# A planned order of loads and blocks for the lead-in of chunked attention with a low-rank mixer and an MLP, replaced by another plan

## Chip, cores and metric

One NeuronCore of one Trainium2 chip. The metric is the device time of one launch in microseconds (us); lower is better.

## What is computed

`q`, `k`, `v` are (8, 8, 576, 64): batch, heads, sequence, head size. Attention runs inside chunks of 64 rows; its output feeds a mixer along the sequence (`U` is 576x32, `V` 32x576) and an MLP (512 to 2048 to 512). The mixer and MLP matrices arrive as 64-bit floats.

```python
scores = scale * np.matmul(q_c, k_c.transpose(0, 1, 2, 4, 3))   # per chunk of 64
attn = np.exp(scores - max) ; attn = attn / (sum + 1e-09)
x = (attn @ v_c)                                # as (batch, seq, 512)
h = x.transpose(0, 2, 1) @ U @ V
u = x + h.transpose(0, 2, 1)
out = u + np.maximum(u @ w_ch1, 0.0) @ w_ch2
```

## The kernel before, in words

Two batches make a pair (four pairs), and the 1152 rows of a pair are nine tiles of 128 rows, `T0` to `T8`. Three tiles are a group; a pair has groups 0, 1 and 2. Tiles 0 to 4 touch the pair's first batch, tiles 4 to 8 its second.

A tile's attention (`attention_ops`, L467): q and k are loaded by SP (L424, L425), v by POOL (L438); PE transposes q and k (L477) and ACT copies them out (L499); PE forms the scores `sc` (L507); VectorE takes maxima (L521) and subtracts (L526); ACT takes the exponential (L536); PE transposes (L477), ACT copies (L499), PE multiplies by v (`av`, L555), and VectorE divides by the sums (L567, L568, L574), which gives `x`.

The mixer: `y` is five products of a batch's `x` with U (L659), rounded to `ys` by ACT and VectorE (L674, L675). Per tile PE forms `u` from `ys` and V (L692), VectorE adds it to `x` (L698), PE transposes (`ut`, L704), ACT and VectorE write the high and low parts `uth` (L724) and `utl` (L729). Group 0 thus needs tiles 0 to 4, group 1 all tiles from 0 to 8.

The MLP runs in blocks. The hidden size is cut into 16 chunks of 128; chunk f has weights `W0` to `W15`. A block (`block_ops`, L801) is one chunk on one group: 12 hidden matmuls `h` (L757), a relu split by ACT (`hh`, L766) and VectorE (`hl`, L771), and 9 output matmuls `o` (L784), three for each of the three tiles, which add up in one PSUM bank per tile over all 16 chunks. Two groups in flight hold six of the eight banks.

A weight chunk arrives as 64-bit words (`wraw`, two transfers of 512 KB by SP, L327 and L331). ACT begins its conversion (L99), VectorE does six steps (L105, L106, L109, L112, L113, L114), ACT writes the high part (L350) and VectorE the low part (L353). The last three chunks are converted in halves. `U` and `V` are converted likewise; `V` also takes a round trip through four transfers by POOL (L296).

The lead-in is pair 0 up to the end of its groups 0 and 1, with the first two tiles of pair 1. Its order isn't written out: `Op` (L126) gives each piece an engine, a duration and a latency, and `order()` (L158) simulates them in time and emits the program in that order, choosing on each engine among the pieces that can start soonest the one with the lowest rank. The ranks come from the lists `LOADS` and `WORK` (L837, L838); `STRETCHES` (L839) is the order of the blocks as (group, first chunk, end chunk). `GATES` (L840) are the counts of blocks after which the first two tiles of pair 1 start; `HALVES_FROM` (L842) is the block from which one transfer a block copies q and k of pair 1 into a second layout (`halve`, L384, 8 for each batch), from which those tiles are then loaded. `begin_filling` and `fill` (L142, L148) put idle matmuls on PE where the plan leaves it without work. Every engine runs its own list strictly in order.

What follows pair 0's group 1 has an order written by hand.

Of the kernel before, what the change touches and what calls it, by code (L numbers as in the profile page):

```python
# [22 lines left out]
def kernel(  # L23
# [25 lines left out]
    GT = 3  # L49
# [108 lines left out]
    def order():  # L158
        free_at = {}
        stock = {k: [0.0] * n for k, n in ROOM.items()}  # L160
# [7 lines left out]
        out = []  # L168
        while ready:
# [29 lines left out]
            for u in users[o]:  # L199
                waits[u] -= 1  # L200
                if not waits[u]:
                    ready[u] = max(p.end + (p.lat if p.eng != u.eng or p.lat > 1 else 0.0) for p in u.after)
            out.append(o)
# [36 lines left out]
    def u_ops():  # L240
# [24 lines left out]

        ld = Op("POOL", 2.7, load, take="w", lat=2.0)
        o, _ = rounding(Later(lambda: st["raw"]), room, ld, "w", 10 * R)
        w = Op("ACT", 1.4, whole, o, take="w", free="w")
        h = Op("ACT", 1.8, high, w)
        lo = Op("DVE", 0.5, low, h, free="w")  # L270
# [7 lines left out]
    def v_ops():  # L278
# [26 lines left out]

        ld = Op("POOL", 0.7, load, take="w", lat=2.5)
        o, _ = rounding(Later(lambda: st["raw"]), room, ld, "w", n)
        o = Op("POOL", 2.4, spread, o, take="w", free="w w", lat=2.5)
        o = Op("ACT", 0.7, high, o)
# [12 lines left out]
    def w_ops(f, after=None):  # L322
# [12 lines left out]
        size = 2 * DM // n  # L335
        ld = Op("SP", 3.2, load, after, take="w", lat=2.0)
        halves = []
# [129 lines left out]
    def attention_ops(pr, t, *after):  # L467
# [102 lines left out]
        def scaled(e):  # L570
# [13 lines left out]
        lq = Op(  # L584
            "SP", 3.4 if own else 5.0, lambda: load_qk(pr, t), *after, take="w" if mine else "qk qk vn", lat=1.6
        )
        if own:
            tq = Op("PE", 0.55, lambda: transpose(src(0), "qT_"), lq, begun.get((pr, t - 2)), take="bank", free="" if mine else "qk")
        else:
            tq = Op("DVE", 1.09, lambda: squares(0, "qT_"), lq, begun.get((pr, t - 2)), take="qk", free="qk")  # L590
        lv = Op(
# [3 lines left out]
            lq,  # L595
            lat=2.2,
        )
# [7 lines left out]
        else:  # L605
            ck = Op("DVE", 1.09, lambda: squares(1, "kT_"), tq, take="qk", free="qk")
            turned = [[tq], [ck]]
# [6 lines left out]
        if own:  # L614
            te = Op("PE", 0.55, lambda: transpose(flat(), "eT_"), ex, take="bank", free=tag_e)
            ce = Op("ACT", 0.58, lambda: evacuate("eT_"), te, take=tag_eT, free="bank")
        else:
            te = Op("SP", 2.5, spread_e, ex, lat=4.0)
            ce = Op("DVE", 1.09, square_e, te, take="eT", free="e")
        av = Op("PE", 0.65, values, ce, lv, take="bank bank x", free=tag_eT + (" w" if mine else " vn"))  # L620
# [11 lines left out]
    def project_ops(pr, e, xs):  # L632
# [168 lines left out]
    def block_ops(pr, g, f, first, final, after, prev):  # L801
# [244 lines left out]
```

## Time and profile before

| | us |
|---|---|
| median of 3 runs | 941.47 |
| lowest and highest | 941.0, 941.57 |
| span of the profiled execution (first to last instruction) | 937.6 |
| PE busy in the span | 916.5 (98%) |
| VectorE busy | 488.7 (52%) |
| ACT busy | 212.3 (23%) |

The page gives the profiled execution's span and no separate time of its own; the median lies 3.9 us above the span. The shares are means over stages with different limits, so the lead-in has to be read by stretches.

### The profile page before, as it was taken

To read this page: it belongs to the slowest core of one execution; us is meant where nothing else is said; L and a number is where in the kernel's file an instruction comes from. 1 tells how busy PE (TensorE), PEld (TensorE's weight loads), DVE (VectorE), ACT (ScalarE), POOL (GpSimd) and SP (SyncE) were. 2 spreads that over 40 slices of the span, in tenths; PEclk is the share of its full clock that TensorE was granted. 3 is DMA by queue.
4 is the path that set the end of the run, shared out by engine and by line. 5 is a ranking of instruction groups with operands and counts; after the bars stand their busy time and mean duration, and the time that the engine had idled before them with its cause. 6 is when DMAs were issued, how large, how long until landed. Compare 5 with 4: busy or idle time off the path is not lost.

```text
span 937.6 us, 16153 instructions
## 1 busy us (share of the span) xinstructions
PE 916.5 (98%) x6639; PEld 806.1 (86%) x6642; DVE 488.7 (52%) x922; ACT 212.3 (23%) x379; POOL 30.1 (3%) x84
## 2 busy tenths in 40 slices
PE   7789999999999999999999999999999999999998
PEld 4569999878898888888898898988889889999997
DVE  6789999975545535553434534553433643321211
ACT  5434343322211212121211221111121211111110
POOL 5510000000000000000000000000000000000000
PEclk9999999999999999999999999999999999999999
DMA  9980688546646535563543733562231512310000
GB/s 214 222 260 1 140 168 185 138 129 146 143 98 150 127 57 130 124 127 81 129 92 79 153 70 79 150 140 68 78 91 35 148 45 46 79 23 1 35 1 34
DMA packets 271449, 98.79 MB, mean 105 GB/s; under 512 B 221296, under 2 KB 257136, under 8 KB 271376
## 3 DMA queue, kind: packets, MB, share of 16 engines
q1 hardware_dynamic: 269440, 94.81, 44.5%
q0 software_dynamic: 1328, 2.80, 1.4%
q8 instruction: 52, 0.85, 0.4%
q10 hardware_dynamic: 608, 0.15, 0.1%
q14 instruction: 21, 0.17, 0.1%
HBM read 73.84 MB, written 37.75 MB: 119 GB/s over the span
## 4 chain that ended last, share of the span: by engine, by line
PE 91%; DMA 3%; DVE 3%; issue 1%; ACT 1%; SPq 0%; POOL 0%; DVEq 0%; ACTq 0%
PE h L757 43%; PE o L784 41%; DMA qkv<-in_q_dram 2%; PE av L555 2%; PE sc L507 2%; PE u L692 1%; PE y L652 1%; PE y L653 1%; DMA vall<-vroom 1%; PE y L659 1%; PE ps_fill L151 0%; DVE eT L463 0%; PE ps_qT L477 0%; DMA us<-us_3d 0%; PE ps_kT L477 0%
## 5 line engine op out<-in xcount | busy, mean ns | idle before, releaser
L757 PE MATMUL h<-uth,w 128*128 128x384 f32 x1536 | 413.5, 337 | 1.6 <-DVE ex L528 1.6
L784 PE MATMUL o<-w,hh 128*128 128x512 f32 x1152 | 346.6, 393 | 0.0
L757 PEld LDWEIGHTS h<-uth,w 128*128 128x128 f32 x1536 | 279.8, 188 | 10.6 <-issue 1.4
L757 PE MATMUL h<-utl,w 128*128 128x384 f32 x768 | 258.1, 336 | 1.3 <-DVE utl L729 1.3
L784 PEld LDWEIGHTS o<-w,hh 128*128 128x128 f32 x1152 | 213.8, 188 | 36.7
L784 PE MATMUL o<-w,hl 128*128 128x512 f32 x576 | 214.2, 396 | 0.0
L771 DVE SCALAR_TENSOR_TENSOR hl<-h,hh 128x384 fp32r<-128x384 f32 x192 | 105.5, 549 | 203.3 <-ACT hh L766 202.8
L766 ACT ACTIVATE hh<-h 128x384 fp32r<-128x384 f32 x192 | 94.4, 491 | 458.7 <-PE h L757 458.5
L757 PEld LDWEIGHTS h<-utl,w 128*128 128x128 f32 x768 | 144.1, 188 | 7.9 <-DVE utl L729 1.6
L784 PEld LDWEIGHTS o<-w,hl 128*128 128x128 f32 x576 | 107.4, 188 | 22.9
L463 DVE STREAM_TRANSPOSE uT<-us 128x512 f32<-128x512 f32 x27 | 29.6, 1097 | 50.7 <-PE h L757 26.9
L463 DVE STREAM_TRANSPOSE eT<-es 128x512 f32<-128x512 f32 x27 | 29.1, 1079 | 41.0 <-DMA es<-es_6d 9.5
L463 DVE STREAM_TRANSPOSE qT<-qn 128x512 f32<-128x512 f32 x27 | 19.1, 709 | 46.4 <-PE h L757 44.7
L536 ACT ACTIVATE ex<-ex 128x512 f32<-128x512 f32 x36 | 22.8, 634 | 72.4 <-DVE ex L528 60.2
L641 ACT CAST xh<-x 128x512 fp32r<-128x512 f32 x30 | 18.5, 618 | 69.7 <-DVE x L574 44.7
L698 DVE TENSOR_TENSOR x<-u,x 128x512 f32<-128x512 f32 x36 | 24.2, 685 | 19.2 <-PE u L692 19.0
L521 DVE TENSOR_REDUCE mx<-sc 128x4 f32<-128x256 f32 x72 | 27.9, 413 | 5.4 <-PE sc L507 5.4
L724 ACT CAST uth<-uT 128x512 fp32r<-128x512 f32 x27 | 16.7, 620 | 53.6 <-DVE uT L463 53.6
L574 DVE TENSOR_TENSOR x<-av,sm 128x256 f32<-128x256 f32 x72 | 27.2, 419 | 1.4 <-DMA out_dram<-x 0.3
L414 POOL MEMSET vn<- 128x8 f32 x27 | 3.1, 114 | 689.1 <-PE av L555 506.3
L796 DVE TENSOR_TENSOR x<-o,x 128x512 f32<-128x512 f32 x36 | 23.1, 677 | 3.6 <-PE o L784 3.6
L645 DVE TENSOR_TENSOR xl<-x,xh 128x512 fp32r<-128x512 f32 x30 | 20.6, 686 | 7.6 <-ACT xh L641 6.8
(85 smaller groups left out, 531.7 us busy)
## 6 DMA issues: line engine op xcount, KB each, us to landing
wraw<-in_moe_w_ch_dram SPq DMA_DIRECT2D x32, 512.0 KB
out_dram<-x SPq DMA_DIRECT2D x36, 256.0 KB
halfq<-in_q_dram SPq DMA_DIRECT2D x24, 288.0 KB
halfk<-in_k_dram SPq DMA_DIRECT2D x24, 288.0 KB
qn<-halfq SPq DMA_DIRECT2D x27, 256.0 KB
kn<-halfk SPq DMA_DIRECT2D x27, 256.0 KB
vn<-in_v_dram SPq DMA_DIRECT2D x108, 64.0 KB
qkv<-in_v_dram POOLq DMA_DIRECT2D x36, 64.0 KB, 7.3
```

The source lines that it names most:

```text
L463: turned = nc.vector.transpose(dst, src)
L507: nc.tensor.matmul(ps[e][cs, hp * C : (hp + 1) * C], lhsT=st["qT_"][rows, hp, cs], rhs=st["kT_"][rows, hp, cs], start=True, stop=True,)
L521: nc.vector.reduce_max(mx, st["sc"][e], axis=AX.X)
L536: nc.scalar.activation(exf, exf, AF.Exp, scale=SCALE)
L574: nc.vector.tensor_mul(by_head[:, heads(pr, t, e), :], st["av"][e][:, :, 0:D], st["sm"][:, e].unsqueeze(2).broadcast_to([P, HP, D]),)
L645: nc.vector.tensor_sub(st["l"], x_of[pr, i + 4 * e], st["h"])
L698: nc.vector.tensor_add(x, st["u"], x)
L757: o = nc.tensor.matmul(ps[:, :GN], lhsT=w[:, z, cc], rhs=u[:, cc, :], start=(n == 0), stop=(n == 3 * NCC - 1))
L766: nc.scalar.activation(hh, ps[:, :GN], AF.Relu)
L771: nc.vector.scalar_tensor_tensor(hl, ps[:, :GN], 0.0, hh, op0=ALU.max, op1=ALU.subtract)
L784: nc.tensor.matmul(acc[g, j], lhsT=h[:, js], rhs=w2[f][:, z], start=(first and i == 0), stop=(final and i == 2),)
L796: nc.vector.tensor_add(x, ps, x)
```

## The change

The program is made by the same planner with other durations, another account of transfers and other lists. No instruction that computes is added or removed; 11 idle matmuls are added in all (53 in place of 42). The core of the diff:

```diff
     class Op:
-        def __init__(self, eng, us, run, *after, take="", free="", lat=0.1):
-            self.eng, self.us, self.run, self.lat = eng, us, run, lat
+        def __init__(self, eng, us, run, *after, take="", free="", lat=0.1, dma=0.0):
+            self.eng, self.us, self.run, self.lat, self.dma = eng, us, run, lat, dma
...
-        free_at = {}
+        free_at = {"SP": 1.85, "POOL": 1.4, "ACT": 3.4, "DVE": 1.5, ("SP", "dma"): 3.9, ("POOL", "dma"): 2.0}
...
-            free_at[o.eng] = end
+            free_at[o.eng] = end - (0.08 if o.eng in ("DVE", "ACT") else 0.0)
+            if o.dma:
+                first = max(t + 1.2, free_at[o.eng, "dma"])
+                other = "SP" if o.eng == "POOL" else "POOL"
+                both = min(o.dma, max(0.0, free_at[other, "dma"] - first))
+                end = free_at[o.eng, "dma"] = first + o.dma + both
+                if both:
+                    free_at[other, "dma"] += both
...
-        ld = Op("SP", 3.2, load, after, take="w", lat=2.0)
+        ld = Op("SP", 1.1, load, after, take="w", dma=3.55, lat=2.2)
...
-    STRETCHES = ((0, 0, 2), (1, 0, 2), (0, 2, 3), (1, 2, 3), (0, 3, 4), (1, 3, 4), (0, 4, 5), (1, 4, 5), (0, 5, 6), (1, 5, 6), (0, 6, 7), (1, 6, 7), (0, 7, 8), (1, 7, 8), (0, 8, 9), (1, 8, 9), (0, 9, 10), (1, 9, 10), (0, 10, 11), (1, 10, 11), (0, 11, 12), (1, 11, 12), (0, 12, 13), (1, 12, 13), (0, 13, 14), (1, 13, 14), (0, 14, 16), (1, 14, 16))
+    STRETCHES = ((0, 0, 4), (1, 0, 1), (0, 4, 5), (1, 1, 6), (0, 5, 6), (1, 6, 8), (0, 6, 8), (1, 8, 11), (0, 8, 9), (1, 11, 12), (0, 9, 16), (1, 12, 16))
-    GATES = (25, 27)
+    GATES = (23, 28)
...
-    HALVES_FROM = 8
+    HALVES_FROM = 16
...
-                Op("SP", 0.6, second.pop(0), prev[0], lat=3.0)
+                halved.append(Op("SP", 0.8, second.pop(0), prev[0], dma=2.75, lat=2.0))
...
-                attention_ops(1, gates[blocks], prev[0])
+                attention_ops(1, gates[blocks], prev[0], *halved[:8])
```

`LOADS` and `WORK` are new lists of the same items, and the loop over `WORK` now makes its pieces in a fixed order and takes only the rank from the list. About twenty durations change by some tenths of a us.

What comes of it on SP, the queue of the early loads: before, W0, T1, T0, T3, T4, W1, T2, T5, T8, W2, T6, T7, W3; now W0, T0, T2, T1, T3, W1, T4, T5, W2, T6, T8, T7, W3. On POOL the round trip of V now stands ahead of all v loads; before, it stood between those of T2 and T5.

On ACT, around the start of the conversion of chunk 2 (`L99`; `ex_5` is the exponential of tile 5, `qkT_6` a copy of tile 6). Before:

```order
L536 ACTIVATE ex_5_604<-ex_5_604 128x512
L299 CAST vst<-vall 128x576
L99 ACTIVATE wroom_675<-wraw_562 128x1024
L499 COPY eT_5_680<-ps_eT_5_667 128x512
L536 ACTIVATE ex_8_672<-ex_8_672 128x512
```

Now:

```order
L543 ACTIVATE ex_3_455<-ex_3_455 128x512
L99 ACTIVATE wroom_558<-wraw_161 128x1024
L506 COPY qkT_5_574<-ps_qT_5_561 128x512
L506 COPY eT_3_578<-ps_eT_3_552 128x512
L506 COPY qkT_5_574<-ps_kT_5_568 128x512
L543 ACTIVATE ex_4_549<-ex_4_549 128x512
L357 CAST w_625<-wroom_389 128x1024
```

Chunk 2 is begun two tiles earlier in the attention, ahead of copies that tiles 3 and 5 need.

On PE, at the first hidden matmul (`y_1` is the second batch's product with U, `u_4` and `ut_4` tile 4's mixer steps). Before:

```order
L659 MATMUL y_1_566<-x_8_794,ust_147 128x512
L704 MATMUL ut_2_949<-ident,x_2_714 128x128 x4
L704 MATMUL ut_3_957<-ident,x_3_441 128x128 x4
L692 MATMUL u_4_964<-ys_0_842,vst 128x512
L692 MATMUL u_4_964<-ys_1_954,vst 128x512
L692 MATMUL u_5_968<-ys_1_954,vst 128x512
L757 MATMUL h_0_0_977<-uth_0_900,w_245 128x384
L757 MATMUL h_0_0_977<-utl_0_901,w_245 128x384
```

Now, the end of the first hidden block, and a piece some rows later:

```order
L771 MATMUL h_0_0_948<-utl_0_865,w_281 128x384
L771 MATMUL h_0_0_948<-uth_0_864,w_281 128x384
L484 MATMUL ps_eT_8_968<-ident,ex_8_908 128x128 x4
L673 MATMUL y_1_906<-x_7_962,ust_142 128x512
L562 MATMUL av_0_8_983<-qkv_8_221,eT_8_977 64x65 x2
```

```order
L798 MATMUL o_0_1002<-w_625,hl_0_1_1046 128x512
L706 MATMUL u_4_1072<-ys_0_784,vst 128x512
L706 MATMUL u_4_1072<-ys_1_1062,vst 128x512
L706 MATMUL u_5_1075<-ys_1_1062,vst 128x512
L798 MATMUL o_1_1011<-w_625,hh_0_1_1041 128x512 x2
L798 MATMUL o_1_1011<-w_625,hl_0_1_1046 128x512
L798 MATMUL o_2_1015<-w_625,hh_0_1_1041 128x512 x2
L798 MATMUL o_2_1015<-w_625,hl_0_1_1046 128x512
L718 MATMUL ut_4_1089<-ident,x_4_714 128x128 x4
L718 MATMUL ut_5_1095<-ident,x_5_796 128x128 x4
```

The first hidden block now stands ahead of the end of tile 8 and of the second batch's mixer, which follow between blocks.

On PE, after the scores of pair 1's first tile. Before:

```order
L507 MATMUL sc_1_0_1939<-kT_0_1928,qT_0_1923 64x64 x2
L757 MATMUL h_1_13_1968<-uth_1_970,w_1801 128x384
L757 MATMUL h_1_13_1968<-utl_1_971,w_1801 128x384
L757 MATMUL h_1_13_1968<-uth_1_970,w_1801 128x384 x2
L757 MATMUL h_1_13_1968<-utl_1_971,w_1801 128x384
```

Now:

```order
L514 MATMUL sc_1_0_1925<-kT_0_1919,qT_0_1910 64x64 x2
L798 MATMUL o_1_1011<-w_1724,hh_0_13_1902 128x512 x2
L798 MATMUL o_1_1011<-w_1724,hl_0_13_1905 128x512
L798 MATMUL o_2_1015<-w_1724,hh_0_13_1902 128x512 x2
L798 MATMUL o_2_1015<-w_1724,hl_0_13_1905 128x512
L771 MATMUL h_0_14_1953<-uth_0_864,w_1786 128x384
```

Output matmuls now stand between the scores and the next hidden block. Chunk 15's first block is the 28th of 32 in place of the 30th. From the third group's third hidden block on, PE's order is the same in both programs.

## Rows read from the trace of the kernel before

**Rows 1.** Busy time by stretch of the span: the columns, then the stretches.

```profile
core 0: us, PE busy (x) PEld busy (x) DVE busy (x) ACT busy (x) POOL busy (x), PEclk, DMA share, GB/s
...
40.00:50.00 10.00, 7.37 (x147) 5.88 (x149) 7.13 (x19) 6.14 (x11) 4.80 (x10) 0.85 1.21 213
...
60.00:68.30 8.30, 6.18 (x52) 3.25 (x51) 7.77 (x16) 3.33 (x6) 0.00 (x0) 1.00 0.61 215
68.30:85.70 17.40, 17.39 (x91) 15.88 (x92) 17.11 (x22) 6.22 (x10) 0.00 (x0) 1.00 0.06 23
85.70:165.00 79.30, 79.30 (x406) 72.51 (x405) 76.10 (x95) 30.29 (x41) 0.00 (x0) 1.00 0.71 147
165.00:182.00 17.00, 16.81 (x112) 14.61 (x110) 15.88 (x30) 5.60 (x11) 0.00 (x0) 1.00 0.66 153
```

**Rows 2.** Timeline of PE at the first hidden matmul: start us, us, what.

```profile
66.71 0.33 PE L757 MATMUL h<-uth,w 128*128 128x384 f32 x1
68.31 0.44 PE L757 MATMUL h<-utl,w 128*128 128x384 f32 x1 [1.26 <-DVE utl L729]
```

**Rows 3.** Who PE waited for: us in total, times, longest us.

```profile
PE h L757 <- DVE ex L528: 1.6, 2, 1.1
...
PE u L692 <- DVE x L698: 0.8, 1, 0.8
```

**Rows 4.** DMA queues, 0 to 39 us (q1 SP, q0 POOL): packets, MB.

```profile
q1 hardware_dynamic: 17028, 6.46, 82.9%
q0 software_dynamic: 808, 1.74, 20.4%
```

**Rows 5.** DMA queue of SP, 0 to 8 us and 0 to 41 us.

```profile
q1 hardware_dynamic: 1785, 1.31, 52.7%
...
q1 hardware_dynamic: 17466, 6.99, 83.2%
```

**Rows 6.** Timeline of ACT: the conversions of chunks 0 and 2 begin.

```profile
9.73 1.12 ACT L99 ACTIVATE wroom<-wraw 128x1024 f32<-128x1024 f32 x1 [2.72 <-DMA wraw<-in_moe_w_ch_dram]
...
44.29 1.12 ACT L99 ACTIVATE wroom<-wraw 128x1024 f32<-128x1024 f32 x1 [2.04 <-DMA wraw<-in_moe_w_ch_dram]
```

**Rows 7.** VectorE by line and shape, 0 to 75 us: count, busy, ns.

```profile
L521 DVE TENSOR_REDUCE mx<-sc 128x4 f32<-128x256 f32 x18 | 7.5, 418 | 4.5 <-PE sc L507 4.4
L574 DVE TENSOR_TENSOR x<-av,sm 128x256 f32<-128x256 f32 x18 | 6.8, 419 | 0.3
...
L698 DVE TENSOR_TENSOR x<-u,x 128x512 f32<-128x512 f32 x6 | 3.8, 680 | 0.0
L109 DVE SCALAR_TENSOR_TENSOR wroom<-wraw,wroom 128x1024 uint32<-128x1024 uint32 x3 | 3.7, 1219 | 0.0
...
L105 DVE TENSOR_SCALAR wroom<-wroom 128x1024 f32<-128x1024 f32 x3 | 2.1, 690 | 1.2 <-ACT wroom L99 1.2
L567 DVE TENSOR_SCALAR sm<-av 128x4 f32<-128x4 f32 x18 | 2.1, 155 | 3.8 <-PE av L555 3.8
L568 DVE RECIPROCAL sm<-sm 128x8 f32<-128x8 f32 x9 | 1.8, 203 | 0.3
```

**Rows 8.** Timeline of VectorE in the dense stretch: two neighbours.

```profile
102.00 1.22 DVE L353 TENSOR_TENSOR w<-wroom,w 128x1024 fp32r<-128x1024 f32 x1
103.13 1.22 DVE L109 SCALAR_TENSOR_TENSOR wroom<-wraw,wroom 128x1024 uint32<-128x1024 uint32 x1
```

**Rows 9.** Timeline of PE, 50 to 67 us: the small products.

```profile
57.56 0.70 PE L555 MATMUL av<-qkv,eT 64*64 64x65 f32 x32
...
59.05 0.60 PE L477 MATMUL ps_eT<-ident,ex 128*128 128x128 f32 x4
...
62.76 1.98 PE L659 MATMUL y<-x,ust 128*128 128x512 f32 x4 [0.47 <-DVE x L574]
...
66.13 0.74 PE L692 MATMUL u<-ys,vst 128*128 128x512 f32 x2 [0.29 <-DVE ys L675]
```

**Rows 10.** Timeline of VectorE: the last steps of chunk 15.

```profile
189.77 1.25 DVE L353 TENSOR_TENSOR w<-wroom,w 128x512 fp32r<-128x512 f32 x2
```

More of the change, by code (lines that the diff above doesn't have):

```diff
@@ L201, in order @@
                 if not waits[u]:
-                    ready[u] = max(p.end + (p.lat if p.eng != u.eng or p.lat > 1 else 0.0) for p in u.after)
+                    ready[u] = max(p.end + (p.lat if p.lat > 0.1 and p.eng != u.eng or p.lat > 1 else 0.1 if "PE" in (p.eng, u.eng) and p.eng != u.eng else 0.03) for p in u.after)
             out.append(o)
@@ L264, in low @@
             nc.vector.tensor_sub(ust[:, :, 3, :], st["u"].bitcast(F32), ust[:, :, 3, :])
-        ld = Op("POOL", 2.7, load, take="w", lat=2.0)
+        ld = Op("POOL", 0.0, load, take="w", lat=5.0)
         o, _ = rounding(Later(lambda: st["raw"]), room, ld, "w", 10 * R)
-        w = Op("ACT", 1.4, whole, o, take="w", free="w")
-        h = Op("ACT", 1.8, high, w)
+        w = Op("ACT", 1.15, whole, o, take="w", free="w")
+        h = Op("ACT", 1.5, high, w)
         lo = Op("DVE", 0.5, low, h, free="w")
@@ L304, in low @@
             nc.vector.tensor_sub(dst, st["all"][rows], dst)
-        ld = Op("POOL", 0.7, load, take="w", lat=2.5)
+        ld = Op("POOL", 0.7, load, take="w", dma=0.6, lat=2.2)
         o, _ = rounding(Later(lambda: st["raw"]), room, ld, "w", n)
-        o = Op("POOL", 2.4, spread, o, take="w", free="w w", lat=2.5)
+        o = Op("POOL", 2.2, spread, o, take="w", free="w w", dma=1.0, lat=2.0)
         o = Op("ACT", 0.7, high, o)
@@ L584, in attention_ops @@
         lq = Op(
-            "SP", 3.4 if own else 5.0, lambda: load_qk(pr, t), *after, take="w" if mine else "qk qk vn", lat=1.6
+            "SP",
+            (1.0 if own else 0.8) * len(list(segments(pr, t))),
+            lambda: load_qk(pr, t),
+            *after,
+            take="w" if mine else "qk qk vn",
+            dma=2.5 if own else 2.3,
+            lat=2.2,
         )
@@ L589, in attention_ops @@
         else:
-            tq = Op("DVE", 1.09, lambda: squares(0, "qT_"), lq, begun.get((pr, t - 2)), take="qk", free="qk")
+            tq = Op("DVE", 0.71, lambda: squares(0, "qT_"), lq, begun.get((pr, t - 2)), take="qk", free="qk")
         lv = Op(
@@ L595, in attention_ops @@
             lq,
-            lat=2.2,
+            dma=1.45,
+            lat=2.0,
         )
@@ L605, in attention_ops @@
         else:
-            ck = Op("DVE", 1.09, lambda: squares(1, "kT_"), tq, take="qk", free="qk")
+            ck = Op("DVE", 0.71, lambda: squares(1, "kT_"), tq, take="qk", free="qk")
             turned = [[tq], [ck]]
@@ L617, in attention_ops @@
         else:
-            te = Op("SP", 2.5, spread_e, ex, lat=4.0)
-            ce = Op("DVE", 1.09, square_e, te, take="eT", free="e")
+            te = Op("SP", 0.7, spread_e, ex, dma=2.0, lat=3.5)
+            ce = Op("DVE", 0.9, square_e, te, take="eT", free="e")
         av = Op("PE", 0.65, values, ce, lv, take="bank bank x", free=tag_eT + (" w" if mine else " vn"))
@@ L676, in out @@
             y_of[pr, e] = y
-        y = Op("ACT", 1.4, out, prev, take="y", free="bank")
+        y = Op("ACT", 0.6, out, prev, take="y", free="bank", lat=0.8)
         steps[-1].append(y)
@@ L815, in out @@
             st[j] = project_out(pr, g, f, (st["hh"], st["hl"]), first, final, j)
-        a = Op("PE", 2.1, h, *after, *(prev[:1] + prev[3:] if prev else ()), take="bank", free="ut" if last else "")
+        a = Op("PE", 2.085, h, *after, *(prev[:1] + prev[3:] if prev else ()), take="bank", free="ut" if last else "")
         a.name = "hidden"
@@ L823, in block_ops @@
         for j in range(GT):
-            d = Op("PE", 0.7, lambda j=j: out(j), c, d, take="bank" if first else "", free="h" if j == GT - 1 else "")
+            d = Op("PE", 0.69, lambda j=j: out(j), c, d, take="bank" if first else "", free="h" if j == GT - 1 else "")
             if final:
@@ L850 @@
     mixed = {}
-    for item in WORK:
-        rank[0] += 1
+    for item in sorted(WORK, key=lambda z: ("UVTWPM".index(z[0]), int(z[1:] or 0))):
+        rank[0] = 1 + WORK.index(item)
         begin = len(ops)
@@ L878 @@
     blocks = 0
+    halved = []
     second = halvings(2) + halvings(3)
```

5 lines of the change are left out of this document (3 added, 2 removed).

## Prediction

> **What bounds the kernel.** The table by stretches comes first [rows 1]. From 85.7 to 165 us PE is busy for all of 79.3 us, so nothing can be won there except by starting earlier; what can be won lies in the 68.3 us before the first hidden block runs, and in the change to pair 1. In the lead-in the DMA engines are full (share 1.21 from 40 to 50 us) and VectorE is not far from it (7.13 of 10 us there, 7.77 of 8.3 us just before 68.3). Then the timeline of PE: the first hidden matmul starts at 66.71, and the second, the first that reads `utl`, waits until 68.31 for VectorE [rows 2]. So VectorE's list up to the third `utl` of group 0 sets the start. Last the waits of PE: two before a hidden block for the subtraction `ex`, 1.6 us, and one of 0.8 us for `x`, all at the entry to pair 1 [rows 3].
>
> The sum is made against the profiled span of 937.6 us; the median of 941.47 lies 3.9 us above it, and I add that back. About 0.2%, 1.9 us, is what a measurement here can tell from no change.
>
> **Term A, the start of the hidden blocks.** Chunk 2 decides it. Ahead of it on SP now stand U, W0, W1 and six tiles (before, seven), so it is complete when SP's queue has moved 6.44 MB; POOL has by then moved the words of V, its round trip and five tiles' v, 1.75 MB. Before, that sum, 8.2 MB, was reached at 39 us [rows 4]. Between the count and the use there is a delay: chunk 2's 6.96 MB were counted by 41 us [rows 5] and ACT began at 44.29, 3.3 us later; chunk 0's 1.19 MB were counted before 8 us and ACT began at 9.73, at least 1.7 us later [rows 5, 6]. I take 2.6, about the middle, and keep both ends. ACT starts at 41.6 and needs 1.1 us: 42.7.
>
> From there VectorE has 46 instructions up to the third `utl`: 21 of the attention's 256-column kind (maxima, subtractions, scalings) at 0.42, 8.8 us; four triples for the sums at 0.51, 2.1; eight of 512 columns (`ys`, four additions, three `utl`) at 0.68, 5.4; three steps of a chunk at 0.69 and two at 1.22, 4.5 [rows 7]. That is 20.8 us of durations. Neighbours that don't depend on each other overlap: the step at 102.00 lasts 1.22 and the next starts 1.13 later [rows 8], 0.09 less. The new list alternates between such neighbours; I count 29 overlaps, 2.6 us, so 18.2. One wait comes on top: behind chunk 2 on ACT stand two copies that tile 3's `av` needs, so that product ends about 1.1 us after VectorE has done its first step. Sum 42.7 + 18.2 + 1.1 = 62.0, against 68.3: **6.3 us earlier**. Ends: with the delay at 1.7 and no wait 60.0 (8.3 earlier); with 3.3 and no overlap at all 65.3 (3.0 earlier).
>
> The Trainium skill's page DMA: Bandwidth & Descriptors (Anatomy of one DMA) puts the fixed part of a DMA, most of it the receipt of the last byte, at about 2.0 us. By that figure ACT would start 0.6 us sooner and the forecast would be 938.2 instead of 938.8. Chunk 2's own row shows 3.3, so the sum stays with rows.
>
> **Term B, what moves behind the first hidden block.** Before, only `ut_4` and `ut_5` came after it. Now also tile 8's transpose of the exponential (0.60), its `av` (0.70), two `y` products (1.98 for four), and three `u` products (0.74 for two) [rows 9]: 0.55 + 0.65 + 1.0 + 0.7, a little under the rows since they overlap, **2.9 us later**. This is work moved, not added; it has to be paid after the start instead of before.
>
> **Term C, new waits among the first blocks.** Before, the stretch from 68.3 to 85.7 is full (17.39 of 17.40 us) [rows 1], so any wait is new. After the third `utl`, VectorE has eight more instructions before tile 8's exponential can start (a subtraction, a 1.14 step of chunk 2, the sums, maximum, scalings): 3.0 us, and ACT 0.65. The hidden block ends 1.9 us after that `utl`, so PE waits 1.75. `u_4` needs `ys_1`, behind chunk 3's step on VectorE: 0.55. `ut_4` and `ut_5` need two additions that stand behind two steps and a relu: 0.8. In all **3.1 us later**. Where the trace has no such row I bound it: 0.5 if VectorE is ahead of my count by one long step each time, 5 if chunk 4's load or conversion is late too.
>
> A + B + C leave 0.3 us at the place that was 85.7 us (four hidden and four output blocks done; now five and three, the same work).
>
> **Term D, the entry to pair 1.** The scores take the two free PSUM banks, and the next hidden block waits until a subtraction frees one: 1.6 us twice, and 0.8 for `u` behind `u` [rows 3]. Now two output groups (1.4 us) and four (2.8 us) stand between, and output products stand between the `u`; a maximum and a subtraction need 0.8 [rows 7]. I take all **2.4 us as gone**; the other end is 0.
>
> Everything else at nothing: the idle matmuls run where PE has no data; the halving transfers, moved from block 8 to block 16, run beside a DMA share of 0.71 [rows 1], and the last of a batch's eight is wanted some 10 us after its issue. If that cover fails, the first tile of pair 1 is late and PE waits at its scores. V's round trip, now early, no longer delays tile 5's v; its cost is already in the 1.75 MB.
>
> Sum: -6.3 + 2.9 + 3.1 - 2.4 = -2.7. Span 934.9, time **938.8 us**.
>
> **Rivals.**
> *More is won.* If chunk 2 lands early and VectorE never waits, A is 8.3; with C at 1.5 the sum is -8.3 + 2.9 + 1.5 - 2.4 = -6.3: 935.2. For it: the new order is built on transfers that share engines, which these rows show. Against it: the delay of chunk 2 in its own row. 0.16.
>
> *The plan doesn't hold, nothing is won.* ACT stands in order behind each chunk's load; the plan placed it where it thought the chunk had landed. If chunk 2 is used 2 us later than I have it, A is 4.3, and the sum -0.7: 940.8; if the entry to pair 1 also keeps its waits, +1.7: 943.2. For it: ACT did wait 2.04 us for chunk 2 before [rows 6]. 0.21.
>
> *Slower: VectorE becomes the bound.* Chunk 15 is now wanted two blocks earlier, and chunks 2 and 3 right behind the start. Before, VectorE ended chunk 15 at 191.0 [rows 10]. Now it is about 5.4 us ahead at the place of 85.7, lays 4.4 us of pair 1's first two tiles and seven relus (3.2) behind, and loses 4.3 us of idle (3.2 and 1.1, [rows 1]): chunk 15 at 173.7, with a relu behind it that PE wants at about 173. There is no room. If half of the some 80 overlaps up to there and half of the 29 before are missed (3.6 and 1.3 us), VectorE is 4.9 us later, and with the 0.7 that is already short the sum is -2.7 + 5.6 = +2.9: 944.4. It decides from about 0.04 us more for each step. Against it: the lists alternate between independent steps more than before. The Trainium skill's page VectorE: DVE Perf Modes (The DRAIN you can't avoid) says that the next instruction doesn't start until the pipe has emptied. By that rule no neighbours overlap, all 109 overlaps at 0.09 are missed, 9.8 us, and the time would be about 949; the 1.13 of [rows 8] speaks against it for independent neighbours, and I give that whole size 0.02 of the 0.13 that slower gets.
>
> **Chances.** Forecast case, 936.9 to 940.9: 0.50, two thirds of it below 939.6. More won 0.16, nothing won 0.21, slower 0.13. Faster by over 0.2%: 0.34 + 0.16 = 0.50; within: 0.16 + 0.21 = 0.37; slower 0.13. The range leaves out the outer part of the first and last rival: 934.5 to 944.5; the forecast case alone has 936.9 to 940.9.
>
> **What would show it.** In the profile after: ACT's start on chunk 2 near 41.6 with a wait on DMA ahead of it; the second hidden matmul near 62; small waits of PE on VectorE, some 3 us together, between there and 86; no wait on `ex` at the entry to pair 1; PE's waits between 86 and 170 near nothing. I am wrong if chunk 2 starts more than 2 us off, if PE waits on `hl` or on a chunk (`w`) in the dense stretch, or if the scores of pair 1's first tile wait for its loads.

## The result and the profile after

The changed kernel takes **949.47 us** (median of 4 runs, 948.7 to 951.01) against 941.24 us for the kernel before (median of 4, 940.02 to 941.57): a ratio of 1.0089, 95% interval 1.0072 to 1.0106. Forecast were 938.8 us and a range of 934.5 to 944.5. The sign is wrong, and the time lies outside the range.

The profiled execution after has a span of 949.2 us and took 951.01 us itself, so 1.8 us lie around the span. The prediction had taken 3.9 us for that distance; by 1.8 us, the profiled execution of before (937.6 us) took 939.4 us and was a short one. The two traces are therefore 11.6 us apart and the medians 8.2.

The stretches of [rows 1] and one behind them, in the kernel after:

```profile
core 0: us, PE busy (x) PEld busy (x) DVE busy (x) ACT busy (x) POOL busy (x), PEclk, DMA share, GB/s
40.00:50.00 10.00, 7.41 (x142) 6.08 (x142) 4.78 (x14) 6.32 (x10) 2.63 (x5) 0.66 1.10 230
60.00:68.30 8.30, 7.71 (x93) 5.38 (x93) 7.79 (x20) 4.46 (x8) 0.11 (x1) 1.00 0.41 120
68.30:85.70 17.40, 17.09 (x114) 13.95 (x113) 16.10 (x26) 7.78 (x11) 0.00 (x0) 1.00 0.35 121
85.70:165.00 79.30, 79.15 (x396) 70.90 (x395) 78.56 (x106) 29.42 (x42) 0.00 (x0) 1.00 0.46 116
165.00:182.00 17.00, 17.00 (x115) 15.07 (x114) 12.80 (x25) 4.82 (x9) 0.11 (x1) 1.00 0.75 109
182.00:210.00 28.00, 24.11 (x175) 20.53 (x174) 14.19 (x29) 5.30 (x10) 0.11 (x1) 0.94 0.69 138
```

From 40 to 50 us, where the forecast let VectorE run through, it is busy for 4.78 us (before: 7.13), and the granted clock of TensorE is 0.66, which between 2.4 and 1.2 GHz means some 6.8 us at the lower level (before, 0.85: 3 us). PE had stood idle for 3.2 us just ahead of it. The timelines of PE and ScalarE say why:

```profile
42.59 1.15 PE L562 MATMUL av<-qkv,eT 64*64 64x65 f32 x32 [3.18 <-ACT eT L506]
```

```profile
34.99 0.63 ACT L543 ACTIVATE ex<-ex 128x512 f32<-128x512 f32 x1 [1.59 <-DVE ex L533]
40.46 1.12 ACT L99 ACTIVATE wroom<-wraw 128x1024 f32<-128x1024 f32 x1 [4.84 <-DMA wraw<-in_moe_w_ch_dram]
41.48 0.58 ACT L506 COPY qkT<-ps_qT 128x512 f32<-128x512 f32 x1
41.94 0.60 ACT L506 COPY eT<-ps_eT 128x512 f32<-128x512 f32 x1
```

ScalarE stands 4.84 us before chunk 2 (2.04 in [rows 6]), and the copies of tiles 3 and 5 that PE and VectorE need stand behind it in its order. At the start of the hidden blocks (the timeline of PE, as in [rows 2]):

```profile
64.83 1.20 PE L562 MATMUL av<-qkv,eT 64*64 64x65 f32 x30 [0.47 <-DMA qkv<-in_v_dram]
...
66.91 0.74 PE L771 MATMUL h<-uth,w 128*128 128x384 f32 x1
67.48 0.34 PE L771 MATMUL h<-utl,w 128*128 128x384 f32 x1
...
89.25 0.62 PE L798 MATMUL o<-w,hh 128*128 128x512 f32 x2
```

The first product that reads `utl` is 0.8 us earlier than before, not 6.3. In the kernel before it started as soon as the third `utl` was written [rows 2]; here it did not wait for it. VectorE's timeline:

```profile
63.35 0.68 DVE L743 TENSOR_TENSOR utl<-ut,uth 128x512 fp32r<-128x512 f32 x1
```

The third `utl` is there at 64.03, and the product that reads it runs 3.45 us later: ahead of it in PE's order stand the rest of a batch's `y`, tile 7's values product `av`, held until 64.83 by the load of v, a transposition and more of `y`. At 89.25 us five hidden and three output blocks are done, the same amount of products as four and four at 85.70 us before.

The third loss is at the entry to pair 1, here on VectorE, ScalarE and PE, one timeline each:

```profile
194.45 0.64 DVE L712 TENSOR_TENSOR x<-u,x 128x512 f32<-128x512 f32 x1
200.58 0.75 DVE L581 TENSOR_TENSOR x<-av,sm 128x256 f32<-128x256 f32 x2 [5.49 <-DMA out_dram<-x]
```

```profile
201.37 0.62 ACT L655 CAST xh<-x 128x512 fp32r<-128x512 f32 x1 [9.40 <-DVE x L581]
201.89 0.48 ACT L780 ACTIVATE hh<-h 128x384 fp32r<-128x384 f32 x1
```

```profile
202.43 1.22 PE L798 MATMUL o<-w,hh 128*128 128x512 f32 x2 [3.89 <-ACT hh L780]
```

VectorE waits 5.49 us until a buffer of pair 0 is stored; ScalarE's next step reads what VectorE writes, a relu stands behind it, and PE waits 3.89 us for that relu. The waits of [rows 3] on `ex` are gone, and this one has taken their place. (The 1.22 for two products is the lower clock again: 0.94 in the stretch.)

To compare programs whose blocks stand in another order I use PE's **lag**: every product counts with its spacing at the full clock (0.1735 us for one of a hidden block, 0.229 for one of an output block, and so on; idle matmuls count nothing), and the lag is how much later than in the profiled execution of before the same sum is reached. It is worked out from all rows of PE, and belongs to one execution of each kernel. At 70 us, where the orders still differ in small products, the spacing taken for those shifts it by some 0.6 us.

| lag in us at | 70 | 100 | 160 | 200 | 260 | 600 | 900 |
|---|---|---|---|---|---|---|---|
| after | 2.9 | 3.6 | 4.9 | 8.0 | 9.5 | 10.8 | 11.6 |

So in these traces the lead-in costs 3.6 us, the dense stretch 1.3, the entry to pair 1 4.6 and the rest 2.

### The profile page after: what moved, and what is told of

It is laid out like the page before. It is cut to its first block, busy times and chain, and to the rows that moved or that the text cites. A ratio compares the mean times of both kernels' runs of the same rounds, so it can differ in the third digit from the quotient of the medians.

```text
span 949.2 us, 16174 instructions
## 1 busy us (share of the span) xinstructions
PE 924.3 (97%) x6653; PEld 810.3 (85%) x6653; DVE 482.9 (51%) x922; ACT 210.4 (22%) x379; POOL 30.2 (3%) x84
## 4 chain that ended last, share of the span: by engine, by line
PE 81%; DMA 6%; DVE 6%; SPq 3%; issue 2%; ACT 1%; POOL 1%; DVEq 0%; ACTq 0%; POOLq 0%
PE h L771 38%; PE o L798 37%; DMA qkv<-in_v_dram 2%; PE av L562 2%; PE sc L514 2%; PE y L666 1%; DVE wroom L109 1%; PE y L667 1%; PE u L706 1%; SPq L461 1%; DVE hl L785 1%; DVE wraw L113 1%; DMA us<-us_3d 1%; DMA vall<-vroom 1%; DVE w L360 1%
## 5 line engine op out<-in xcount | busy, mean ns | idle before, releaser
L562 PEld LDWEIGHTS av<-vn,eT 64*64 64x64 f32 x864 | 15.8, 134 | 12.0 <-issue 12.0
```

Source lines behind the costliest of these rows:

```text
L562: nc.tensor.matmul(ps[e][cs, hp * D1 : (hp + 1) * D1], lhsT=st["eT_"][rows, hp, cs], rhs=vn[rows, c, hp, :], start=True, stop=True,)
```

## The experiments

Times are medians; the ratio is to the kernel before, run on the same chip in turn. The planner makes its order anew for each edit, so most edits move more than the line that they change; where that matters, the text says how many of PE's 5443 matmul instructions (idle ones not counted) stand elsewhere in the program, as a comparison of the two lists counts them.

| run | what | us | ratio, 95% |
|---|---|---|---|
| e1_halves8 | after, halving transfers from block 8 | 946.09 | 1.0054, 1.0039 to 1.0069 |
| e2_chunk2_later | after, chunk 2 planned to land later | 951.63 | 1.0106, 1.0088 to 1.0123 |
| e3_both | e1 and e2 | 948.41 | 1.0081, 1.0062 to 1.0100 |
| e4_before_halves16 | before, halving transfers from block 16 | 949.98 | 1.0093, 1.0076 to 1.0111 |
| e5_v7_early | e3, v of tile 7 earlier | 944.23 | 1.0026, 1.0013 to 1.0038 |
| e6_no_chunk2_edit | e5 without e2's edit | 946.67 | 1.0062, 1.0048 to 1.0076 |
| e7_lists_alone | after, block order, gates and halving as before | 948.56 | 1.0071, 1.0054 to 1.0088 |
| e8_stretches_alone | before, new block order | 948.34 | 1.0078, 1.0060 to 1.0096 |
| e9b_pairs_from_6 | e5, old block order from the 13th block | 942.46 | 1.0015, 1.0003 to 1.0028 |
| e9c_three_then_two | e5, another block order | 944.48 | 1.0038, 1.0022 to 1.0054 |
| e10_vector_relief | e9c, a VectorE step on GpSimd | 961.63 | 1.0203, 1.0180 to 1.0227 |
| e11_before_relief | before, the same | 965.84 | 1.0266, 1.0238 to 1.0293 |
| e12_one_step_less | e9c, a VectorE step left out | 941.15 | 0.9992, 0.9973 to 1.0011 |
| e13_before_one_step_less | before, the same | 950.52 | 1.0095, 1.0079 to 1.0112 |
| e14_step_less_same_order | as e12, order kept | 943.52 | 1.0034, 1.0021 to 1.0046 |
| e15_before_step_less_same_order | as e13, order kept | 941.55 | 1.0008, 0.9994 to 1.0023 |

### The entry to pair 1: the halving transfers on SyncE's queue

```diff
-    HALVES_FROM = 16
+    HALVES_FROM = 8
```

> The changed kernel with one number put back: the halving transfers of q and k of the next pair start after block 8 again and not after block 16. Theory S (SyncE's queue): from block 16 on these 16 transfers stand on SyncE's queue between the loads and the stores of the entry to pair 1; the stores of pair 0's first three tiles go out late, VectorE waits 5.5 us for a buffer they hold, and ScalarE, PE and PE's clock follow. Between the 24th and the 40th hidden block the changed kernel lost 4.4 us against the kernel before. Expected: that wait of VectorE and the 3.9 us of PE on ScalarE are gone, and the time is 949.5 - 4.4 = 945 (943.5 to 946.5). Rival V (the new order of blocks, with chunk 15 wanted at the 28th block, loses it through VectorE): no change, 948.5 to 950.5.

Measured: 946.09 us. That is 3.4 us less than the changed kernel. The edit also moves 171 matmuls and 32 of VectorE's instructions. VectorE's wait for the store and PE's for the relu are gone, and the lag stays where it was: 4.4 us at 170, 5.2 at 260 (after: 5.1 and 9.5). The opposite edit in the kernel before:

```diff
-    HALVES_FROM = 8
+    HALVES_FROM = 16
```

> The kernel before with one number changed: the halving transfers start after block 16 and not after block 8. Theory S: the same loss at the entry without any other part of the change, 941.3 + 4.4 = 945.5 (943.5 to 947.5), with a wait of VectorE on the stores. Rival V: no change, 940.5 to 942.5, since the order of blocks is that of before.

Measured: 949.98 us, 9 us slower and more than expected. PE's order is untouched by this edit, VectorE's and ScalarE's differ in one place; what moves is SyncE's order. The lag is 0.2 us up to 190 us and 9.2 from 210 us on. VectorE's longest wait between 190 and 225 us:

```profile
DVE x L574 <- DMA out_dram<-x: 7.2, 1, 7.2
```

So theory S holds, and with the orders of PE and VectorE nearly fixed this is its cleanest run. In e4 SyncE also stood 3.6 us (before: 1.9) for a round trip of tile exponentials that stands ahead of the stores in its order, and issued the first store at 205.3 us instead of 198.8; how much of that is the full queue and how much SyncE's own order isn't separated. On SyncE's queue the changed kernel had four halving transfers between the loads of pair 1's first tile and the first three stores; e1, like before, has none there. The queue of SyncE from 176 to 200 us (packets, MB, share of 16 engines), after and then e1:

```profile
q1 hardware_dynamic: 12047, 3.30, 70.0%
```

```profile
q1 hardware_dynamic: 3922, 2.44, 33.8%
```

Three times the packets and twice the share of the DMA engines for 1.35 times the bytes: the size of these transfers does not tell what they cost the queue. What e1 did not show is a gain at the entry. Its waits there:

```profile
PE av L562 <- issue: 1.4, 2, 1.2
PE sc L514 <- DVE kT L470: 0.8, 1, 0.8
PE u L706 <- DVE x L712: 0.8, 1, 0.8
```

Together 3.0 us, where the kernel before has 2.4 [rows 3]: the waits on `ex` went, others came.

### The lead-in: two holds

```diff
-        ld = Op("SP", 1.1, load, after, take="w", dma=3.55, lat=2.2)
+        ld = Op("SP", 1.1, load, after, take="w", dma=3.55, lat=6.5 if f == 2 else 2.2)
```

> The changed kernel with one number of the planner changed: it takes chunk 2 to land 4.3 us later, and so puts ScalarE's first step on chunk 2 behind seven other ScalarE steps (the copies of tiles 3, 4 and 5, an exponential, the conversion of chunk 0). Loads stand as in the changed kernel. Theory A (ScalarE's queue): the 4.84 us that ScalarE stood before chunk 2 held the copies, left PE idle for 3.2 us, took its clock down for 6.8 us and left VectorE 4.8 of 10 us busy between 40 and 50 us; without it the first hidden product with utl starts near 63.5 instead of 67.5, and the time is 945.5 (944 to 947.5). Rival D (the loads set the start: tiles 6 to 8 land late whatever ScalarE does): the start stays at 66.5 or later, and the time at 948.5 to 950.5.

> Both edits of the two runs before together. By S and A the two losses lie in different stretches and add: 949.5 - 4.4 - 4 = 941 (939 to 943.5). If one of the two theories falls, the time is that of the other edit alone, 945 to 946; if both, 949.

Measured: 951.63 and 948.41 us, no gain; theory A alone falls. The edit does not move ScalarE's step alone: 179 matmuls stand elsewhere in e2 than in the changed kernel (78 in e3 against e1). The 4.84 us were gone, yet the first hidden block of e2 started at 65.89. Its timeline shows the next thing in the way, the v of tile 7:

```profile
62.42 0.33 PE L562 MATMUL av<-qkv,eT 64*64 64x65 f32 x2
64.57 0.83 PE L562 MATMUL av<-qkv,eT 64*64 64x65 f32 x30 [1.82 <-DMA qkv<-in_v_dram]
...
65.89 0.98 PE L771 MATMUL h<-uth,w 128*128 128x384 f32 x1
```

In the changed order of loads tile 7 comes last, and each tile's v waits for the transposes of q of the tile loaded before it, here tile 8. The next edit takes tile 6's:

```diff
     for a, b in zip(tiles_in, tiles_in[1:]):
+        a = 6 if b == 7 else a
         ahead[b] = a
```

> The kernel of e3_both with one edge of the plan moved: the loads of tile 7's v no longer wait for tile 8's transposes of q, but for tile 6's. In e2_chunk2_later and e3_both PE stood 1.8 and 2.1 us before tile 7's values product for that load, right ahead of the first hidden block, with all three utl ready. Theory D (that load sets the start): the wait goes, the first hidden block starts near 64.2 instead of 66.2, and the time is 948.4 - 2 = 946.4 (945.5 to 947.5). Rival W (VectorE, 19.7 of 20 us busy in each stretch from 80 to 160 us, sets the place at 170 us whatever the start): 948 to 949.

> The changed kernel with the halving transfers from block 8 on and tile 7's v no longer behind tile 8's q, but with ScalarE's first step on chunk 2 where the change put it: the kernel of e5_v7_early without the edit of e2. Theory A2 (the two things in the lead-in hide each other: ScalarE's wait before chunk 2 and the late v of tile 7 each alone hold the start at 66 us): 946 (945 to 947.5), start at 66 or later. Rival D alone (only the v load mattered): as e5_v7_early, 943.5 to 945.

Measured: 944.23 and 946.67 us. With e1 and e3 these make a square, all with the halving transfers from block 8. Behind each time stand, from the profiled execution, when the third `utl` was written and when the first product that reads it started:

| | v of tile 7 late | v of tile 7 early |
|---|---|---|
| without e2's edit | 946.09 (e1): 64.50, 67.77 | 946.67 (e6): 63.40, 66.17 |
| with e2's edit | 948.41 (e3): 61.42, 67.27 | 944.23 (e5): 62.21, 65.11 |

Either edit alone gains nothing, both gain 1.9 us over e1. What the v of tile 7 costs is shown: from e3 to e5 only 5 matmuls and 6 of VectorE's instructions move, the product starts 2.2 us earlier, and the time falls by 4.2 us. From e1 to e3 the `utl` came 3.1 us earlier and the product only 0.5: the v stood in the way. What ScalarE's wait costs by itself is not shown. From e6 to e5 99 matmuls move, and e6's own trace has a wait of 1.00 us before chunk 2 (and 6.23 before chunk 1); its lag is e5's at 70 us and 2.6 us larger at 90, with a wait of PE of 1.3 us for a relu in between.

### Lists and block order belong together

The changed lists with the old block order (`STRETCHES`, `GATES` and `HALVES_FROM` of before), and the new `STRETCHES` alone in the kernel before:

> The changed planner and its lists of loads and work, with the kernel before's order of blocks, gates and start of the halving transfers. Theory L (the loss of 3.6 us by 70 to 100 us comes from the lists: the order of loads, conversions and tiles ahead of the start): the loss stays, 944.5 to 947. Theory Q (it comes from the new order of blocks, four of group 0 first, which wants chunk 3 by the fourth block): gone, 940 to 942.5.

> The kernel before with the new order of blocks alone; planner, lists, gates and start of the halving transfers as before. Theory Q: the loss comes with it, 944 to 946.5, in waits of PE on chunks or their last VectorE step between 70 and 100 us. Theory L: 940 to 943, and if the entry to pair 1 gains from output groups between its scores and subtractions, 1 to 2 us less than 941.

Measured: 948.56 and 948.34 us. Both theories were put too simply: each half loses by itself, and in the traces between 70 and 90 us, where the lag goes from -0.1 to 6.1 us (e7) and from 1.9 to 9.0 (e8). PE's longest waits from 60 to 85 us in e7:

```profile
PE ut L718 <- DVE x L712: 1.8, 1, 1.8
PE h L771 <- ACT uth L738: 0.7, 1, 0.7
```

and from 66 to 95 us in e8:

```profile
PE h L757 <- ACT w L350: 1.3, 1, 1.3
PE h L757 <- DVE utl L729: 1.3, 1, 1.3
PE h L757 <- DVE w L353: 0.7, 1, 0.7
```

e7 wants group 1's `ut` before its lists have them; e8 wants chunk 3 before the old lists have it (its wait on `utl` stands in the kernel before too [rows 2]). These waits are less than half of what is lost; TensorE's clock takes a part of the rest, 0.71 from 80 to 90 us in e7 and 0.82 from 66 to 95 us in e8, where the kernel before has 1.00 [rows 1]. Each half costs some 7 us by itself and both together, with the new gates, 5 (e1; all three halve from block 8): the losses don't add, and neither half can be judged without the other.

### What an early start is worth

Two other block orders on top of e5, with the gates of before; for e9b:

```diff
-    STRETCHES = ((0, 0, 4), (1, 0, 1), (0, 4, 5), (1, 1, 6), (0, 5, 6), (1, 6, 8), (0, 6, 8), (1, 8, 11), (0, 8, 9), (1, 11, 12), (0, 9, 16), (1, 12, 16))
-    GATES = (23, 28)
+    STRETCHES = ((0, 0, 4), (1, 0, 1), (0, 4, 5), (1, 1, 6), (0, 5, 6), (0, 6, 7), (1, 6, 7), (0, 7, 8), (1, 7, 8), (0, 8, 9), (1, 8, 9), (0, 9, 10), (1, 9, 10), (0, 10, 11), (1, 10, 11), (0, 11, 12), (1, 11, 12), (0, 12, 13), (1, 12, 13), (0, 13, 14), (1, 13, 14), (0, 14, 16), (1, 14, 16))
+    GATES = (25, 27)
```

and for e9c:

```diff
-    STRETCHES = ((0, 0, 4), (1, 0, 1), (0, 4, 5), (1, 1, 6), (0, 5, 6), (1, 6, 8), (0, 6, 8), (1, 8, 11), (0, 8, 9), (1, 11, 12), (0, 9, 16), (1, 12, 16))
-    GATES = (23, 28)
+    STRETCHES = ((0, 0, 3), (1, 0, 2), (0, 3, 4), (1, 2, 4), (0, 4, 5), (1, 4, 5), (0, 5, 6), (1, 5, 6), (0, 6, 7), (1, 6, 7), (0, 7, 8), (1, 7, 8), (0, 8, 9), (1, 8, 9), (0, 9, 10), (1, 9, 10), (0, 10, 11), (1, 10, 11), (0, 11, 12), (1, 11, 12), (0, 12, 13), (1, 12, 13), (0, 13, 14), (1, 13, 14), (0, 14, 16), (1, 14, 16))
+    GATES = (25, 27)
```

> The kernel of e5_v7_early with the order of blocks of the kernel before from the 13th block on (one block of each group in turn) and its gates. Between 110 and 170 us e5_v7_early lost 1.4 us more against the kernel before, VectorE 19.7 of 20 us busy, waits of PE on hl. Theory W (VectorE: the new order wants chunks 10 to 15 one or two blocks earlier): the 1.4 us come back, less the entry's own waits of before (which the new order saves or not: 0 to 2.4), 942 to 944.5. Rival (the loss in that stretch is a debt of the first ten blocks): 944 to 945.5.

> The kernel of e5_v7_early with another order of blocks from the start: three of group 0, two of group 1, one and two, then in turn as before, and the gates of before. Chunk 3 is wanted by the sixth block and not by the fourth, group 1's utl by the fourth and not by the fifth. Theory W: less is asked of VectorE early, the drift of 2.2 us from 70 to 150 us goes, 941.5 to 943.5. Rival Q2 (group 1 begins before its tiles are through, as in e7_lists_alone): a wait of 2 to 5 us of PE before group 1's first block, 945 to 948.

Measured: 942.46 and 944.48 us; e9b is the best version of the changed planner that does all the work, still 0.15% behind the kernel before. The telling one is e9c. In its profiled execution, which took 942.63 us and so was a short one, the start is where the prediction had put it:

```profile
61.79 0.74 PE L771 MATMUL h<-uth,w 128*128 128x384 f32 x1
62.37 0.34 PE L771 MATMUL h<-utl,w 128*128 128x384 f32 x1
```

and its lag is -2.2 us at 70 us, -1.1 at 100, +0.5 at 160. The gain is given back while PE looks busy. (Three more executions of this lead-in start some 3 to 4 us later, see the last section.) The suspect was VectorE; six runs went into it. First a step of chunks 4 to 15 on GpSimd:

```diff
-                nc.vector.tensor_sub(st["w"][:, 1, cols], v, st["w"][:, 0, cols])
+                (nc.gpsimd if f >= 4 else nc.vector).tensor_sub(st["w"][:, 1, cols], v, st["w"][:, 0, cols])
```

> The kernel of e9c_three_then_two with the last VectorE step of chunks 4 to 15 (1.2 us for a whole chunk) run on GpSimd, which is idle then: 12 chunks, some 14.6 us taken off VectorE between 70 and 172 us. Theory W (what the early start won is given back between 70 and 150 us because VectorE, 19.7 of 20 us busy, serves hl late): of the 2.6 us lost there most come back, 941 to 943 against 944.5. Rival X (GpSimd needs far longer for a step, or slows VectorE while it runs; chunks come late): 945 to 950. Rival Y (the drift is not VectorE's): 944 to 945.5.

> The kernel before with the same edit, as a control. There PE waits for nothing between 85 and 165 us, so by theory W nothing can be won in that stretch: 940 to 942, at most 1.6 us less where the subtractions of pair 1's first scores come sooner. Rival X: slower than 942.5, in waits of PE on chunks or hl.

Measured: 961.63 and 965.84 us. Rival X holds, see the last section; VectorE was not relieved, so theory W was not tried. Then the last addition of the rounding left out for the same chunks, whose weights then lack their low words:

> The kernel of e9c_three_then_two with one VectorE step of each of chunks 4 to 15 left out (the addition of the low words: 1.2 us for a whole chunk, 12 chunks, some 14.6 us); these weights lack their low words. Nothing runs on GpSimd in its place. Theory W (VectorE, busy 19.7 of 20 us, gives the early start back between 70 and 150 us): the 2.6 us lost there come back, 941 to 943 against 944.5, and PE's waits on hl between 80 and 150 us are gone. Rival Y (the drift is not VectorE's): 944 to 945.5, and the same waits.

> The kernel before with the same step left out, as a control. PE waits for nothing there between 85 and 165 us: by theory W 940 to 941.5, at most 1.6 us less at the entry to pair 1. If this kernel gains 2 us or more as well, what e12 gains says nothing of the early start.

Measured: 941.15 and 950.52 us. The first is what W expects, but the control lost 9.3 us: with that step at no cost the planner wrote another order (222 matmuls and 52 of VectorE's instructions stand elsewhere; in e12, against e9c, 246 and 48), and the trace loses 4.9 us between 120 and 160 us and 8.6 between 200 and 220, there with a wait of PE of 4.1 us for a transposition of VectorE. So the same 15 instructions were left out with the plan unchanged:

```diff
+            if f >= 4:
+                o.run = lambda: None
```

> The kernel of e9c_three_then_two without the addition of the low words of chunks 4 to 15, as in e12, but the plan keeps the step with its time, so that the order on every engine is that of e9c word for word and only 15 VectorE instructions are missing. Theory W: the drift of 2.6 us between 70 and 150 us goes, 941 to 943 against 944.5; rival Y: 944 to 945.5.

> The kernel before without the same 15 instructions, the order on every engine kept word for word: the control that e13, whose plan was made anew, was not. Theory W: nothing to win where PE waits for nothing, 939.5 to 941.5. If it is 945 or more, as e13 was (950.5), less work on VectorE alone makes the kernel slower, through buffers that come free early and loads that start early; then e13's loss is not the new order's.

Measured: 943.52 and 941.55 us. The control stands still, as it should (1.0008, 0.9994 to 1.0023), and e13's loss was its order's. e14's time is not to be told from e9c's (1.0034 and 1.0038, the intervals overlap); what the step is worth shows in the traces. The stretches 100 to 120 and 120 to 140 us of e9c, then of e14:

```profile
100.00:120.00 20.00, 19.60 (x99) 17.50 (x99) 19.67 (x25) 8.30 (x10) 0.00 (x0) 1.00 0.68 121
120.00:140.00 20.00, 19.79 (x99) 17.30 (x98) 19.75 (x24) 7.60 (x10) 0.00 (x0) 1.00 0.87 209
```

```profile
100.00:120.00 20.00, 20.00 (x102) 18.11 (x101) 16.74 (x22) 7.89 (x11) 0.00 (x0) 1.00 0.70 155
120.00:140.00 20.00, 20.00 (x103) 18.27 (x102) 17.51 (x21) 6.53 (x10) 0.00 (x0) 1.00 0.87 176
```

With VectorE at 17 instead of 19.7 of 20 us, PE gets 102 and 103 matmuls through instead of 99, and the lag grows by 0.3 us from 100 to 160 us instead of 1.6. That fits VectorE taking some 1.3 us of the early start back, but does not show it: e14's execution had no early start (lag 3.0 us at 100 us, e9c's -1.1), and with all steps and a late start the loss is small too, 0.5 us in e1 (lag 3.9 at 100 us, VectorE busy for 58.7 of 60 us), while e12, without the steps, loses 1.0. Nor is it shown that the kernel's time follows. The other 1.1 us, between 70 and 100 us, e14 loses too. That part is in both traces a wait of 0.7 us of a hidden block on `utl` and some that the views don't name; it stays open.

## Why the prediction was wrong

Its terms, beside what the traces show:

| term | forecast | measured |
|---|---|---|
| A, first product that reads `utl` | -6.3 | -0.8 (68.31 to 67.48) |
| B and C, from there to the place of 85.7 us | +6.0 | +4.4 (21.77 us instead of 17.39) |
| dense stretch, after that | 0 | +1.3 |
| D, entry to pair 1 | -2.4 | +4.6 |
| the rest | 0 | +2.0 |

**Term A** fails twice, and the first is the sentence that "VectorE's list up to the third `utl` of group 0 sets the start". It set it in the kernel before. After the change the third `utl` was written at 64.03 and PE reached the product at 67.48: 3.45 of the 5.5 us that are missing are PE's own order, which now has tile 7's v product, a transposition and `y` in front. The sum has no term for them. In e5, without the two holds, the product still comes 2.9 us after the `utl`.

The other 2.0 us fail at the sentence that lets VectorE run from chunk 2 to the third `utl` with "one wait" on top, 1.1 us: on the way VectorE waited 4.3 us on PE and ScalarE, 3.2 more, and chunk 2 gave 1.1 of it back. Chunk 2 itself was near: ScalarE began it at 40.46, forecast 41.6. Two misses offset each other there: the 8.2 MB were counted between 37 and 38 us, not at 39, and the use came some 3 us later, not 2.6. (The 2.0 us of the Trainium skill's page DMA: Bandwidth & Descriptors, Anatomy of one DMA, stand in a section on transfers issued by GpSimd; SyncE issued this one, and with some 3 us the trace doesn't agree with them.) But ScalarE had waited 4.84 us for it with copies behind, so PE stood idle for 3.2 us and VectorE for 2.0 and 1.4, and TensorE's clock fell (0.66 from 40 to 50 us). I counted how long VectorE's 46 instructions last and what stood behind chunk 2 on ScalarE, and not what the wait in front of it does to everything that feeds VectorE. Tile 7's v was treated as bytes (1.75 MB on POOL's queue) and not as a load with a gate. Without these two holds the product starts at 65.11 (e5), 64.82 (e9b) and, with e9c's order, between 62.37 and 66.53: the forecast's 62.0 was nearly reached in one execution, and what holds the others is open but for what the last section shows.

**Terms B and C** were mis-sized against each other. PE's only wait of note in those 22 us is 0.30 us, on `x`, where I had 3.1 for C. The other 4.1 us stand against the 2.9 of B: by their starts the pieces that moved take 3.2 us (four `y` matmuls moved, not two), and 0.9 lie in small gaps.

**Term D** fails twice. "Everything else at nothing" costed the halving transfers by the DMA engines' share (0.71 in [rows 1]) and named only the loads of the tile as what they could delay. They stood on SyncE's queue ahead of the stores, and VectorE waited for the buffer of a store: 3.4 us by e1, 9 by e4. And the 2.4 us of waits did not go even without that; others of 3.0 us took their place.

**The rest** (2 us, in small waits between 500 and 750 us) comes in part from the short profiled execution of before: e15, whose program is before's with 15 instructions less, has a lag of 2.1 us at 600 us.

**The rivals.** The time lies near the 949 us that the third rival gave for the rule of the Trainium skill (VectorE: DVE Perf Modes, The DRAIN you can't avoid). That is chance. The section itself excepts a next instruction that isn't held, and that is what neighbours do here too (in the kernel after a step of 1.21 us begins at 46.30 and the next at 47.43). By the rival's mechanism VectorE would have been late with chunk 15; it ended its last step on it here [rows 10]:

```profile
174.35 1.29 DVE L360 TENSOR_TENSOR w<-wroom,w 128x512 fp32r<-128x512 f32 x2 [0.69 <-ACT w L357]
```

at 175.6 us, where the forecast had 173.7, and PE waited for nothing there. "The plan doesn't hold" described the lead-in, but took it for the end of the loss and gave it 943.2 at most; the store behind the halving transfers was in no rival. None of the three signs of being wrong appeared either: chunk 2 was 1.1 us off, PE waited for nothing from 85.7 to 165 us, and the scores of pair 1's first tile did not wait for their loads.

## What to carry to other kernels

When an early piece gets ready sooner, read in the order of the engine that uses it what else stands in front: here it was ready 3.45 us before its use. Where a load moves on a queue that also carries stores, list what is behind it on that queue and which buffer waits for each of those, down to the engine that stands in front of that buffer: the share of the DMA engines says nothing about it. An in-order engine that waits for a late load is a loss for everything behind it; removing one hold shows little while the next one ends at the same time, so take them away in pairs before calling either harmless, and keep the order of everything else where you can. And an order that was found as a whole is judged as a whole: halves of it, and even a kernel with less work whose order was made anew, lost 7 to 9 us here.

## What the runs showed of the hardware that was not expected

**Steps of GpSimd and VectorE stop each other.** In e10 the subtraction of 128x1024 takes GpSimd 2.63 us in the mean, and VectorE's steps beside it grow. GpSimd's and then VectorE's timeline at two such places:

```profile
98.12 3.43 POOL L360 TENSOR_TENSOR w<-wroom,w 128x1024 fp32r<-128x1024 f32 x1 [5.97 <-ACT w L357]
105.79 2.38 POOL L360 TENSOR_TENSOR w<-wroom,w 128x1024 fp32r<-128x1024 f32 x1 [4.24 <-ACT w L357]
```

```profile
98.06 1.22 DVE L109 SCALAR_TENSOR_TENSOR wroom<-wraw,wroom 128x1024 uint32<-128x1024 uint32 x1
99.20 0.55 DVE L789 SCALAR_TENSOR_TENSOR hl<-h,hh 128x384 fp32r<-128x384 f32 x1
99.67 2.43 DVE L112 TENSOR_SCALAR wraw<-wroom 128x1024 uint32<-128x1024 uint32 x1
...
105.98 3.27 DVE L109 SCALAR_TENSOR_TENSOR wroom<-wraw,wroom 128x1024 uint32<-128x1024 uint32 x1
```

At 98 us VectorE was first, and GpSimd's step lasts 3.43 us instead of 2.4; the step that VectorE begins meanwhile, at 99.67, takes 2.43 us instead of 0.69 and ends after GpSimd's too. At 105.8 us GpSimd was first, and VectorE's step, 1.22 us otherwise, ends 1.1 us after GpSimd's. Not every step is hit: the relu's part at 99.20, which reads `h` from PSUM, takes its usual 0.55 us. No wait shows in any view: the steps themselves are longer (L109 has a mean of 2522 ns in e10 from 90 to 160 us, 1217 in e9c). The Trainium skill's page SBUF — State Buffer (SBUF: two separate sides) says that the two share a pair of ports as an exclusive lock, held for a whole instruction, and that a VectorE step takes it with two inputs in SBUF or in a two-port mode; these rows agree.

**The same order, another lead-in.** e9c and e14 have the same order up to 83.9 us, where the first left-out step would stand, and their profiled executions have a lag of -2.2 and +2.0 us at 70 us (they took 942.63 and 946.9 us themselves). The first product that reads `utl` starts at 62.37 us in e9c, and at 65.51, 65.89 and 66.53 in e10, e12 and e14, whose lead-ins have its order too. Most of the difference between e9c and e14 arises here on PE, e9c first:

```profile
42.01 0.63 PE L484 MATMUL ps_qT<-ident,qkv 128*128 128x128 f32 x4 [0.99 <-DMA qkv<-in_q_dram]
...
44.57 1.98 PE L673 MATMUL y<-x,ust 128*128 128x512 f32 x4
```

```profile
43.42 0.63 PE L487 MATMUL ps_qT<-ident,qkv 128*128 128x128 f32 x4 [1.47 <-DMA qkv<-in_q_dram]
...
46.73 3.78 PE L676 MATMUL y<-x,ust 128*128 128x512 f32 x4
```

The load came later in e14, and behind it TensorE ran at its lower level: the granted clock from 40 to 50 us is 1.00 in e9c, 0.71 in e14 and 0.68 in e12, which had waited 1.64 us for that load. In e10 it is 1.00 there, but 0.83 from 30 to 40 and from 50 to 60 us (e9c: 0.85 and 1.00), with a wait of 1.83 us for a load of k. One trace of a lead-in that is full of transfers is uncertain by some 4 us, about as much as this change was meant to win.
